# Transposing softmax weights in seven blocks of 128 keys over two heads instead of eight blocks of 112

## The chip, the cores and the metric

The kernel runs on one core of a Trainium2 chip. Its engines are named as in the profile: PE (TensorE, matrix products) with its weight loads PEld, DVE (VectorE), ACT (ScalarE), POOL (GpSimd) and SP (SyncE, which here only issues transfers). The metric is the device time of one launch in microseconds (us), where lower is better.

## The reference, cut to what matters

Attention over 4 batches of 12 heads with 448 tokens and 64 dimensions a head, then two MLP blocks. Everything is float32.

```python
q_n, k_n = (rmsnorm(q, g_q), rmsnorm(k, g_k))          # over the 64 dimensions of a head
scores = scale * np.matmul(q_n, k_n.transpose(0, 1, 3, 2))
scores = scores - np.max(scores, axis=-1, keepdims=True)
attn = np.exp(scores)
attn = attn / (np.sum(attn, axis=-1, keepdims=True) + 1e-09)
attn_out = np.matmul(attn, v)                          # (4, 12, 448, 64)
x = attn_out.transpose(0, 2, 1, 3).reshape(B, S, H * D)
# then: x + relu(layernorm(x) * g_ln @ w_ch1) @ w_ch2, and a gated MLP with a product over tokens
```

## The kernel before, in words

The program has three stages on the time axis: attention, the first MLP (`ph` and `pm` products, L781 and L804), and the gated MLP. Attention works on 24 pairs of heads. A head's 448 tokens are split in 4 chunks of 112 rows (`CP, NCH = 112, 4`): token 4p + c stands in row p of chunk c, for queries, keys and values alike.

For a pair i, numbered in the tile names, PE, ACT and DVE do this:

- `pk`, `pq` (L526): four transposes each bring the normalized k and q of both heads to 128 rows (2 heads of 64 dimensions) by 448 tokens; ACT copies them out as `kT`, `qT` (L535).
- `s` (L550): for each query chunk c, the scores of 112 queries against 448 keys, one product for each head, which run side by side on the two halves of PE's rows. DVE takes the row maximum (`nmx`, L556), ACT the exponential into `P`, one tile of 112 x 448 for each head and chunk, with the row sums (L560).
- `t` (L584): the weights `P` are transposed, so that keys lie on partitions. For each head j there are 4 blocks of 112 keys and 4 query chunks: 32 transposes for a pair, in 4 groups of 8 (`t00`, `t01`, `t10`, `t11`: first digit the half of the keys, second the head). Each group fills two PSUM banks and is copied out as `PT`, three groups by ACT (L114) and one by DVE (L594).
- `po` (L601): 8 products of v (112 keys x 64 dimensions) with `PT`, 4 key blocks for each head, the two heads side by side on the two halves of PE's columns.
- `px`, `x`, `pxT`, `y`: the result is copied (`OT`), transposed back, divided by the row sums on DVE (L640), kept for the layer norm's statistics (`lnst`), transposed again and copied to `y`.

POOL squares and normalizes the next pairs' q and k (`sq`, `kq`, L421 to L487). SP loads k, q (two pairs at a time) and v (L506, one transfer a pair into one of two `vr` buffers).

The code does not write the instructions out in a loop: `op(...)` records each step with a place number, an engine, an assumed cost and what it reads and writes, and `arrange` (L296) then emits them. PE's steps are emitted strictly in the order of their place numbers; the others go to whichever ready step comes first by the assumed times. The place numbers come from `ORDER` (the PE steps of a pair and how many pairs they run ahead or behind), `BEHIND` (places of the other engines' steps relative to those), and `EARLY`, single corrections by step and pair, which before exist for pairs 0 to 3 alone. PE changes between three ways of working: the full array (F: all transposes), two row halves (R: `s`) and two column halves (C: `po`). `FILL` (L69) adds products of the identity with itself ahead of some steps near the start, whose results are overwritten.

PSUM has three two-bank buffers `s` for `s` and `t`, and two one-bank buffers `x` for the rest.

Of the kernel before, what the change touches and what calls it, by code (L numbers as in the profile page):

```python
# [39 lines left out]
def attention_mlp_gated(ctx, tc, q, k, v, g_q, g_k, g_ln, w1, w2, w_in, w_sp, b_sp, w_out, out):  # L40
# [437 lines left out]
    def plan_norm(i, n0):  # L478
# [15 lines left out]
        for z, nm in enumerate(("k", "q")):  # L494
            hs = (2 * j, 2 * j + 1)
            r = [f"{nm}r{g}"] + [f"{x}{h}" for x in (f"{nm}r{g}_", f"rq{g}_{nm}") for h in hs]
            w = {"w": [f"kq{i}", f"kn{i}"], "new": "ws"} if z == 0 else {"w": [f"qn{i}"]}
            op(n0 + 2 * z, e, f, lambda nm=nm: norm(nm), r=r + ([f"kq{i}"] if z else []), **w)

    def plan_v(i, n0):  # L500

# [880 lines left out]
```

## Time and profile before

| what | value |
|---|---|
| median of 3 runs | 1213.06 us (1211.55 to 1213.32) |
| the profiled execution's own time | 1213.73 us |
| its span in the profile | 1211.9 us |
| busy in the span: PE, PEld | 1197.6 us, 1023.7 us |
| busy in the span: DVE, ACT, POOL | 765.8 us, 460.6 us, 301.9 us |
| granted PE clock over the run | 0.998 |

The span runs from the first instruction to the last. Busy time counts instructions that do work. PE's products are pipelined, and the end of one in the profile lies after the start of the next, so how fast PE goes is read from one group's start to the next one's, not from an instruction's own duration.

### The profile page before, as it was taken

Reading aid. Unit: us, or ns where it says so; the run is one execution under the profiler, and the core shown is the slowest. Engines: PE = TensorE matmul, PEld = TensorE weight load, DVE = VectorE, ACT = ScalarE, POOL = GpSimd, SP = SyncE. Lnnn points to the kernel's source line nnn. Section 1 sums busy time; section 2 is a strip of 40 time slices with the busy share of each in tenths; the row PEclk is TensorE's granted clock in tenths of the full one; section 3 lists DMA queues with packets and bytes.
Section 4 is the critical chain, followed back from the end, with each engine's and each line's share of the span. In section 5 each row is a group of like instructions: output and inputs, shape, how many; then the busy total and the mean of one; then the engine's idle time right before and its main releaser. Section 6 shows DMA issues by size and latency. Waiting matters only on the chain.

```text
span 1211.9 us, 16730 instructions
## 1 busy us (share of the span) xinstructions
PE 1197.6 (99%) x6568; PEld 1023.7 (84%) x6568; DVE 765.8 (63%) x1398; ACT 460.6 (38%) x918; POOL 301.9 (25%) x275
## 2 busy tenths in 40 slices
PE   8999999999999999999999999999999999999998
PEld 6565656657899999999999999999999988989888
DVE  6888898987888666665758576756445573241240
ACT  4788888997423222222213131322212031223122
POOL 4754767633111101010202010111111003140200
PEclk9999999999999999999999999999999999999999
DMA  4212112111214342323322223233010219102103
GB/s 111 74 54 78 53 54 67 60 42 42 78 53 145 116 133 67 130 77 114 104 87 93 90 104 104 104 109 101 27 52 2 103 67 324 46 1 75 39 1 92
DMA packets 59855, 99.26 MB, mean 82 GB/s; under 512 B 11584, under 2 KB 47808, under 8 KB 59520
## 3 DMA queue, kind: packets, MB, share of 16 engines
q1 hardware_dynamic: 59168, 95.44, 24.9%
q10 hardware_dynamic: 608, 2.75, 0.6%
q8 instruction: 52, 0.85, 0.3%
q14 instruction: 27, 0.22, 0.1%
HBM read 78.88 MB, written 19.30 MB: 81 GB/s over the span
## 4 chain that ended last, share of the span: by engine, by line
PE 91%; DVE 4%; ACT 2%; DMA 2%; POOL 1%; issue 0%; POOLq 0%; ACTq 0%; SPq 0%
PE ph L781 29%; PE pm L804 28%; PE s L550 5%; PE po L601 5%; PE gp L1042 5%; PE gv L888 5%; PE gu L936 5%; PE t L584 4%; PE gs L963 2%; ACT P L560 1%; DVE nmx L556 1%; DMA kr<-in_k_dram 1%; DVE y L812 1%; PE pq L526 1%; PE pxT L656 1%; PE px L635 1%
## 5 line engine op out<-in xcount | busy, mean ns | idle before, releaser
L804 PE MATMUL pm<-h,ws 128*128 128x448 f32 x1728 | 361.4, 362 | 0.0
L781 PE MATMUL ph<-xn,ws 128*128 128x448 f32 x1728 | 360.9, 362 | 0.3 <-DVE y L812 0.3
L804 PEld LDWEIGHTS pm<-h,ws 128*128 128x128 f32 x1728 | 323.8, 188 | 22.3 <-issue 0.7
L781 PEld LDWEIGHTS ph<-xn,ws 128*128 128x128 f32 x1728 | 323.8, 188 | 22.1 <-DVE y L812 0.5
L244 POOL TENSOR_TENSOR ws<-wc,ws 128x768 fp32r<-128x768 f32 x48 | 91.8, 1912 | 570.3 <-ACT ws L114 545.0
L812 DVE TENSOR_TENSOR y<-pm,y 128x448 f32<-128x448 f32 x318 | 176.2, 614 | 56.2 <-PE pm L804 56.2
L791 ACT ACTIVATE h<-ph 128x448 fp32r<-128x448 f32 x96 | 51.8, 539 | 256.0 <-PE ph L781 255.5
L796 DVE SCALAR_TENSOR_TENSOR h<-ph,h 128x448 fp32r<-128x448 f32 x96 | 59.6, 621 | 117.2 <-ACT h L791 116.2
L560 ACT ACTIVATE P<-s,nmx 112x448 f32<-112x448 f32 x192 | 119.3, 637 | 33.5 <-DVE nmx L556 31.3
L556 DVE TENSOR_REDUCE nmx<-s 112x2 f32<-112x896 f32 x96 | 101.2, 1083 | 22.2 <-PE s L550 22.0
L584 PE MATMUL t<-ident,P 112*112 112x112 f32 x768 | 88.9, 260 | 2.4 <-ACT P L560 1.8
L104 ACT ACTIVATE wc<-wr 128x768 f32<-128x768 f32 (+1 forms) x64 | 54.8, 859 | 94.0 <-DMA wr<-in_moe_w_ch_dram 49.3
L114 ACT ACTIVATE ws<-wc 128x768 fp32r<-128x768 f32 x48 | 40.5, 844 | 118.5 <-PE ph L781 92.0
L550 PE MATMUL s<-kT,qT 64*112 64x448 f32 x384 | 85.2, 563 | 0.0
L584 PEld LDWEIGHTS t<-ident,P 112*112 112x112 f32 x768 | 76.6, 133 | 7.6 <-ACT P L560 5.3
L601 PE MATMUL po<-PT,vr 112*64 112x448 f32 x384 | 77.6, 545 | 0.0
L105 DVE TENSOR_SCALAR wc<-wc 128x768 f32<-128x768 f32 (+1 forms) x64 | 40.6, 638 | 50.3 <-ACT wc L104 49.9
L114 ACT ACTIVATE PT<-t 112x896 f32<-112x896 f32 x72 | 66.2, 931 | 4.5 <-PE t L584 2.8
L601 PEld LDWEIGHTS po<-PT,vr 112*64 112x64 f32 x384 | 26.4, 136 | 47.2 <-issue 45.6
L107 DVE SCALAR_TENSOR_TENSOR wc<-wr,wc 128x768 int32<-128x768 int32 (+1 forms) x64 | 64.4, 1010 | 1.5
L108 DVE SCALAR_TENSOR_TENSOR wc<-wr,wc 128x768 uint32<-128x768 uint32 (+1 forms) x64 | 62.5, 977 | 1.6
L550 PEld LDWEIGHTS s<-kT,qT 64*112 64x112 f32 x384 | 30.6, 173 | 37.0 <-issue 21.9
(166 smaller groups left out, 1240.5 us busy)
## 6 DMA issues: line engine op xcount, KB each, us to landing
wr<-in_moe_w_ch_dram SPq DMA_DIRECT2D x48, 768.0 KB, 4.4
wr<-in_moe_w_in_dram SPq DMA_DIRECT2D x12, 512.0 KB, 3.7
win_dram<-wr SPq DMA_DIRECT2D x12, 512.0 KB, 2.6
vr<-in_v_dram SPq DMA_DIRECT2D x24, 224.0 KB, 2.7
kr<-in_k_dram SPq DMA_DIRECT2D x11, 448.0 KB, 4.0
qr<-in_q_dram SPq DMA_DIRECT2D x11, 448.0 KB, 4.7
wr<-in_moe_w_out_dram SPq DMA_DIRECT2D x4, 768.0 KB, 5.0
wout_dram<-wr SPq DMA_DIRECT2D x4, 768.0 KB, 3.2
```

The lines of the kernel that those rows point to most:

```text
L107: lambda: v.scalar_tensor_tensor(ci, hi, -0x40000000, ci, op0=ALU.bitwise_and, op1=ALU.bitwise_or),
L108: lambda: v.scalar_tensor_tensor(cu, lo.bitcast(U32), 29, cu, op0=ALU.logical_shift_right, op1=ALU.bitwise_or),
L114: nc.scalar.activation(d, s, AF.Copy)
L244: nc.gpsimd.tensor_tensor(t[:, 1], pl["c"], f32(t[:, 0]), op=ALU.subtract)
L550: nc.tensor.matmul(p[:CP, j, :S], pr["qT"][rows, c * CP : (c + 1) * CP], pr["kT"][rows], start=True, stop=True)
L556: nc.vector.tensor_reduce(t, pr["s", c][:CP, :, :S], axis=AX.X, op=ALU.max, negate=True)
L560: nc.scalar.activation(t, pr["s", c][:CP, j, :S], AF.Exp, bias=pr["m", c][:, j : j + 1], scale=1.0, accum_out=pr["sum"][:, j, c : c + 1],)
L584: nc.tensor.transpose(p[:CP, e, c * CP : (c + 1) * CP], pr["P", j, c][:, kc * CP : (kc + 1) * CP], ident[:CP, :CP])
L601: nc.tensor.matmul(pr["po"][j * D : (j + 1) * D, :S], raw["v", i][:, j, kc, :], pr["PT", kc // 2, j][:, kc % 2], start=(kc == 0), stop=(kc ...
L781: nc.tensor.matmul(hid[u, b][0][:, :S], s1[:, a, kk, :], xn[b][:, c, kk, :], start=(kk == 0 and m == 0), stop=(kk == NK - 1 and m == 2),)
L804: nc.tensor.matmul(po[:, :S], s2[:, a, m * P : (m + 1) * P], hs[:, c, :], start=(first and e == 0), stop=(last and e == 2),)
L812: nc.vector.tensor_tensor(y[b][:, m, :], po[:, :S], y[b][:, m, :], op=ALU.add)
```

## The change

The keys of a pair's two heads are put side by side: `P` becomes one tile of 112 queries x 896 keys for each chunk, where each head's exponential fills one half. The 896 keys are cut in 7 windows of 128 instead of 8 of 112: windows 0 to 2 belong to the first head, 4 to 6 to the second, and window 3 holds the first head's last 64 keys and the second head's first 64. A pair takes 28 transposes instead of 32, each from 112 x 128 to 128 x 112. They stand in four groups: windows 0 and 1, 5 and 6, 2 and 4 (this one copied by DVE), and window 3 alone (a copy of 448 columns instead of 896, by ACT).

`po` keeps its 8 products: three windows for each head, and window 3 once for each head, with v rows that are zero where the keys are the other head's. The zeros are written once, into two `vr` buffers that stay; after that a pair's v is loaded by 4 transfers instead of 1, in rows of 64 numbers instead of 256. So that keys come in token order, the four transposes of k write every fourth column of `pk`. The `P` pool has 7 tiles of double size instead of 14. `ORDER`, `BEHIND`, `FILL` and the places of `plan_rms` and `plan_norm` get other numbers, and `EARLY` now has corrections for all 24 pairs.

```diff
-    FILL = {"pq0": 22, "s0_3": 5, "s0_0": 4, "pk1": 12, "s1_0": 3}
+    FILL = {"pq0": 22, "s0_1": 3, "s0_3": 15, "t0_0_0": 3, "pk2": 4}
...
-    ORDER = "po-1 s3+1 pq+2 t00 px-1 t11 pk+2 t10 pxT-1 t01 s2+1 s0+1 s1+2".split()
+    ORDER = "po-1 s3+1 pk+2 t10 px-1 t01 pq+2 t11 t00 pxT-1 s2+1 s0+1 s1+2".split()
...
-            raw["v", i] = ap["vraw"].tile([CP, 2, NCH, D], F32, tag="vr", name=f"vr{i}")
-            nc.sync.dma_start(
-                raw["v", i].rearrange("p h c d -> p h (c d)"),
-                v[b, 2 * hp : 2 * hp + 2].rearrange("h (p c) d -> p h (c d)", c=NCH),
-            )
-
+            t = raw["v", i] = vrs[i % 2]
+            for j in range(2):
+                of = v[b, 2 * hp + j]
+                nc.sync.dma_start(t[j * D : (j + 1) * D, j, 3], of[(1 - j) * 3 * P : (1 - j) * 3 * P + D])
+                nc.sync.dma_start(t[:, j, :3], of[j * D : j * D + 3 * P].rearrange("(w p) d -> p w d", p=P))
...
-                    p[:, c * CP : (c + 1) * CP],
+                    p[:, c:S:NCH] if nm == "k" else p[:, c * CP : (c + 1) * CP],
...
+        WINDOWS = {(0, 0): (0, 1), (0, 1): (5, 6), (1, 0): (2, 4), (1, 1): (3,)}
...
-            for e in range(2):
-                kc = 2 * half + e
+            for e, w in enumerate(WINDOWS[half, j]):
                 for c in range(NCH):
                     nc.tensor.transpose(
-                        p[:CP, e, c * CP : (c + 1) * CP], pr["P", j, c][:, kc * CP : (kc + 1) * CP], ident[:CP, :CP]
+                        p[:, e, c * CP : (c + 1) * CP], pr["P", c][:, w * P : (w + 1) * P], ident[:CP, :CP]
                     )
...
-            for kc in range(NCH):
+            for z in range(NCH):
                 for j in range(2):
+                    w = 3 if z == NCH - 1 else 4 * j + z
                     nc.tensor.matmul(
                         pr["po"][j * D : (j + 1) * D, :S],
-                        raw["v", i][:, j, kc, :],
-                        pr["PT", kc // 2, j][:, kc % 2],
-                        start=(kc == 0),
-                        stop=(kc == NCH - 1),
+                        raw["v", i][:, j, w - 4 * j if z < NCH - 1 else 3],
+                        pr["PT", w],
+                        start=(z == 0),
+                        stop=(z == NCH - 1),
                     )
```

The instructions on PE for the transposes of pair 12, where the first number after a tile's name is the pair. Before, this group (second half of the keys, second head) has eight rows, between `px11` and `pk14`:

```order
L635 MATMUL px11_2243<-ident_64,OT11_2218 112x128 x4
L584 MATMUL t12_1_1_2254<-ident_64,P12_0_1_2197 112x112
L584 MATMUL t12_1_1_2254<-ident_64,P12_1_1_2052 112x112
L584 MATMUL t12_1_1_2254<-ident_64,P12_2_1_2188 112x112
L584 MATMUL t12_1_1_2254<-ident_64,P12_3_1_2101 112x112
L584 MATMUL t12_1_1_2254<-ident_64,P12_0_1_2197 112x112
L584 MATMUL t12_1_1_2254<-ident_64,P12_1_1_2052 112x112
L584 MATMUL t12_1_1_2254<-ident_64,P12_2_1_2188 112x112
L584 MATMUL t12_1_1_2254<-ident_64,P12_3_1_2101 112x112
L526 MATMUL pk14_2267<-ident_64,kq14_1961 128x112 x4
```

In the changed kernel the group of that name holds window 3 alone and has four rows; it now stands last of the four groups, behind `pxT11`:

```order
L737 MATMUL pxT11_2208<-ident_64,x11_2167 128x112 x4
L658 MATMUL t12_1_1_2217<-ident_64,P12_0_2123 128x112
L658 MATMUL t12_1_1_2217<-ident_64,P12_1_1965 128x112
L658 MATMUL t12_1_1_2217<-ident_64,P12_2_2114 128x112
L658 MATMUL t12_1_1_2217<-ident_64,P12_3_2019 128x112
L619 MATMUL s13_2_2227<-kT13_2009,qT13_2059 112x448 x2
```

The other three groups keep eight rows, with results of 128 x 112 instead of 112 x 112. Over the program the `t` rows fall from 768 to 672; the other products of PE are as many as before (its identity fills 47 instead of 46), and PE changes its way of working 104 times between the first and the last of the attention's steps instead of 103. From the end of attention on, PE's order is the same in both.

ACT's rows around the copies of pair 12, before:

```order
L114 ACTIVATE PT12_0_0_2272<-t12_0_0_2232 112x896
L535 ACTIVATE kT14_2293<-pk14_2267,gk_c_69 128x448
L114 ACTIVATE PT12_1_0_2304<-t12_1_0_2274 112x896
L114 ACTIVATE PT12_0_1_2315<-t12_0_1_2295 112x896
L114 ACTIVATE y1_1540<-pxT11_2288 128x448
```

and in the changed kernel, where the third copy has half the columns:

```order
L114 ACTIVATE PT12_0_1_2194<-t12_0_1_2176 128x896
L604 ACTIVATE qT14_2213<-pq14_2189 128x448
L114 ACTIVATE PT12_0_0_2223<-t12_0_0_2196 128x896
L114 ACTIVATE PT12_1_1_2234<-t12_1_1_2217 128x448
L114 ACTIVATE y1_1506<-pxT11_2208 128x448
```

DVE keeps one copy of 896 columns for each pair. At the start of the program PE's rows up to the second pair's first scores were these before (`pq0` to `s1_0`):

```order
L73 MATMUL s0_3_221<-ident_64 128x128 x5
L550 MATMUL s0_3_221<-kT0_214,qT0_210 112x448 x2
L550 MATMUL s0_2_233<-kT0_214,qT0_210 112x448 x2
L550 MATMUL s0_1_239<-kT0_214,qT0_210 112x448 x2
L73 MATMUL s0_0_254<-ident_64 128x128 x4
L550 MATMUL s0_0_254<-kT0_214,qT0_210 112x448 x2
L73 MATMUL pk1_300<-ident_64 128x128 x12
L526 MATMUL pk1_300<-ident_64,kq1_288 128x112 x4
L526 MATMUL pq1_324<-ident_64,kq1_288 128x112 x4
```

and are these in the changed kernel:

```order
L73 MATMUL s0_1_229<-ident_64 128x128 x3
L619 MATMUL s0_1_229<-kT0_222,qT0_219 112x448 x2
L619 MATMUL s0_0_239<-kT0_222,qT0_219 112x448 x2
L619 MATMUL s0_2_245<-kT0_222,qT0_219 112x448 x2
L73 MATMUL s0_3_282<-ident_64 128x128 x15
L619 MATMUL s0_3_282<-kT0_222,qT0_219 112x448 x2
L595 MATMUL pk1_305<-ident_64,kq1_258 128x112 x4
L595 MATMUL pq1_312<-ident_64,kq1_258 128x112 x4
L73 MATMUL t0_0_0_331<-ident_64 128x128 x3
```

The fills ahead of the fourth scores rise from 4 to 15, the 12 ahead of `pk1` are gone, and two groups of pair 0's transposes now come before the second pair's scores instead of behind two of them.

## Rows read from the trace of the kernel before

**Rows 1.** Windows of the program: busy time of each engine and granted clock.

```profile
core 0: us, PE busy (x) PEld busy (x) DVE busy (x) ACT busy (x) POOL busy (x), PEclk, DMA share, GB/s
0.00:46.00 46.00, 38.39 (x254) 28.28 (x254) 32.93 (x78) 25.70 (x59) 25.85 (x35) 0.96 0.37 96
46.00:303.00 257.00, 255.60 (x1783) 158.41 (x1784) 219.95 (x473) 219.21 (x521) 149.58 (x145) 1.00 0.20 58
312.00:1212.00 900.00, 894.99 (x4491) 830.87 (x4489) 506.79 (x833) 213.45 (x337) 126.19 (x96) 1.00 0.27 89
```

**Rows 2.** Chain of work that ended last, 100 to 126 us: start, us, what.

```profile
105.45 3.16 PE po L601 x16
108.61 0.94 PE s L550 x4
...
111.29 0.77 PE t L584 x8
112.06 0.38 PE pk L526 x4
112.44 0.77 PE t L584 x8
113.21 0.38 PE pxT L656 x4
113.59 0.77 PE t L584 x8
114.36 2.44 PE s L550 x12
116.80 3.16 PE po L601 x16
```

**Rows 3.** The same chain, products with v: the second pair's and the 22nd's.

```profile
48.48 3.16 PE po L601 x16
...
280.94 3.16 PE po L601 x16
```

**Rows 4.** Groups of instructions by form, 46 to 303 us: count, busy, mean.

```profile
L584 PE MATMUL t<-ident,P 112*112 112x112 f32 x704 | 81.4, 260 | 1.2 <-ACT P L560 1.0
L114 ACT ACTIVATE PT<-t 112x896 f32<-112x896 f32 x66 | 60.9, 932 | 4.3 <-PE t L584 2.5
L594 DVE COPY PT<-t 112x896 f32<-112x896 f32 x23 | 24.9, 1085 | 1.7 <-PE t L584 0.9
L114 ACT ACTIVATE OT<-po 128x448 f32<-128x448 f32 x22 | 12.5, 567 | 0.0
```

**Rows 5.** Weight loads on PE in order of time, 157 to 161 us.

```profile
157.86 0.82 PEld L584 LDWEIGHTS t<-ident,P 112*112 112x112 f32 x8
158.64 0.43 PEld L526 LDWEIGHTS pk<-ident,kq 112*128 112x128 f32 x4
159.03 0.81 PEld L584 LDWEIGHTS t<-ident,P 112*112 112x112 f32 x8
159.79 0.43 PEld L656 LDWEIGHTS pxT<-ident,x 112*128 112x128 f32 x4
160.18 0.81 PEld L584 LDWEIGHTS t<-ident,P 112*112 112x112 f32 x8
```

**Rows 6.** Transfers by line: count, KB each, median us to landing.

```profile
vr<-in_v_dram SPq DMA_DIRECT2D x24, 224.0 KB, 2.7
wr<-in_moe_w_spatial_dram SPq DMA_DIRECT2D x16, 56.0 KB, 2.3
```

**Rows 7.** PE in order of time near the start, idle time before in brackets.

```profile
16.75 2.08 PE L73 MATMUL s<-ident 128*128 128x128 f32 x8 [2.02 <-ACT P L560]
...
20.38 2.94 PE L73 MATMUL pk<-ident 128*128 128x128 f32 x24
```

**Rows 8.** Waits, 46 to 303 us: who for whom, us in total, times, longest.

```profile
PE t L584 <- ACT P L560: 1.0, 2, 0.7
...
ACT P L560 <- DVE nmx L556: 20.1, 21, 2.1
...
DVE nmx L556 <- PE s L550: 19.5, 27, 1.8
```

More of the change, by code (lines that the diff above doesn't have):

```diff
@@ L276, in at @@
     def at(nm, i):
-        return 8 * i + AT[nm] + EARLY.get((nm, i), 0)
+        return 8 * i + AT[nm] + EARLY.get(nm, {}).get(i, 0)
     def op(n, eng, us, fn, r=(), w=(), new=None, mode=None):
@@ L497, in plan_norm @@
             w = {"w": [f"kq{i}", f"kn{i}"], "new": "ws"} if z == 0 else {"w": [f"qn{i}"]}
-            op(n0 + 2 * z, e, f, lambda nm=nm: norm(nm), r=r + ([f"kq{i}"] if z else []), **w)
+            op(
+                n0 + 2 * z + EARLY.get(("KQkq", "KQqn")[z], {}).get(i, 0), e, f, lambda nm=nm: norm(nm), r=r + ([f"kq{i}"] if z else []), **w,
+            )
+    vrs = []
     def plan_v(i, n0):
@@ L504, in load @@
         def load():
-            raw["v", i] = ap["vraw"].tile([CP, 2, NCH, D], F32, tag="vr", name=f"vr{i}")
-            nc.sync.dma_start(
-                raw["v", i].rearrange("p h c d -> p h (c d)"),
-                v[b, 2 * hp : 2 * hp + 2].rearrange("h (p c) d -> p h (c d)", c=NCH),
-            )
+            t = raw["v", i] = vrs[i % 2]
[3 more added lines that the diff above has]
+                nc.sync.dma_start(t[:, j, :3], of[j * D : j * D + 3 * P].rearrange("(w p) d -> p w d", p=P))
+        if i < 2:
+            vrs.append(ap["vraw"].tile([P, 2, NCH, D], F32, tag=f"vr{i}", name=f"vr{i}"))
+            for j in range(2):
+                nc.gpsimd.memset(vrs[i][(1 - j) * D : (2 - j) * D, j, 3], 0.0)
         dma(n0 - 2, 229, load, w=[f"vr{i}"], new="vr")
@@ L574, in plan_pair @@
             for j in range(2):
-                r = ["s" + o, "nmx" + o, f"ssum{i}"]
-                op(at(f"P{c}", i), "ACT", 0.62, lambda c=c, j=j: s_exp(c, j), r=r, w=[f"P{o}_{j}"], new="P")
+                r = ["s" + o, "nmx" + o, f"ssum{i}"] + ["P" + o] * j
+                w, new = ([f"P{o}_1"], None) if j else (["P" + o, f"P{o}_0"], "P")
+                op(at(f"P{c}", i), "ACT", 0.62, lambda c=c, j=j: s_exp(c, j), r=r, w=w, new=new)
+        WINDOWS = {(0, 0): (0, 1), (0, 1): (5, 6), (1, 0): (2, 4), (1, 1): (3,)}
+        DVE_COPY = (1, 0)
         def t_pe(half, j):
@@ L611, in plan_pair @@
                 o, n = f"{i}_{half}_{j}", at(f"t{half}{j}", i)
-                r = [f"P{i}_{c}_{j}" for c in range(NCH)]
-                op(n, "PE", 0.77, lambda half=half, j=j: t_pe(half, j), r=r, w=["t" + o], new="s", mode="F")
-                eng, us = ("DVE", 1.08) if half and j else ("ACT", 0.92)
+                r = [f"P{i}_{c}{x}" for c in range(NCH) for x in ["", "_0", "_1"] if x != f"_{1 - j}" or half]
+                us = 0.385 if half and j else 0.77
+                op(n, "PE", us, lambda half=half, j=j: t_pe(half, j), r=r, w=["t" + o], new="s", mode="F")
+                eng = "ACT" if (half, j) != DVE_COPY else "DVE"
+                us = (0.56, 0.56) if half and j else (0.92, 1.08)
+                us = us[eng == "DVE"]
                 op(at(f"PT{half}{j}", i), eng, us, lambda half=half, j=j, eng=eng: t_out(half, j, eng), r=["t" + o], w=["PT" + o], new="PT")
@@ L647, in ln_stats @@
         def ln_stats(cs):
-            if hp == 0 and 0 in cs:
+            if b not in lnst:
                 lnst[b] = lnp.tile([CP, NCH, NPAIR, 6], F32, tag="lnst", name=f"lnst{b}", bufs=3)
@@ L658, in xT_act @@
         def xT_act():
-            if hp == 0:
+            if b not in y:
                 y[b] = y_a.tile([P, NK, S], F32, tag="y", name=f"y{b}")
```

38 lines of the change are left out of this document (25 added, 13 removed), and 59 rows, old and new, of tables (BEHIND, EARLY).

## Prediction

> **What bounds the kernel now.** I read the windows of the program first [rows 1]. From 46 to 303 us, where attention runs steadily, PE is busy 255.60 of 257.00 us at a granted clock of 1.00, while DVE and ACT are busy 219.95 and 219.21 us, about 85% each. From 312 us to the end PE is busy 894.99 of 900.00 us. So PE sets the time nearly everywhere, and only the first 46 us hold much else (38.39 us busy there, part of it fills). A busy PE is not proof, since its durations overlap, so I then took the chain that ended last and read distances between starts. Between two products with v that follow each other without a gap it holds PE's work alone: 105.45 to 116.80 us, 11.35 us for one pair [rows 2]. Over 20 pairs, from the second pair's product with v at 48.48 us to the 22nd's at 280.94 us, the mean is 232.46 / 20 = 11.62 us [rows 3]. Three batches end in that stretch, each with eight more transposes for the layer norm, at 0.38 us for four like those of pk [rows 2]: 3 x 0.76 = 2.3 us. 20 x 11.35 + 2.3 = 229.3 us, so PE's waits are worth about 232.5 - 229.3 = 3.2 us in 20 pairs. That is the whole that a better order could win in the steady part. Whatever takes work off PE in each pair is therefore worth its full size, as long as the engines behind it keep pace.
>
> **The transposes.** A group of eight takes 0.77 us on the chain [rows 2], 0.096 us for one. (The 260 ns mean of one [rows 4] is latency and must not be multiplied.) Four fewer for each of 24 pairs are 96 x 0.096 = 9.2 us. That needs a transpose with 128 weight columns to go as fast as today's with 112. The trace has such transposes: pk and pxT load 112 x 128, and the next group starts 0.39 us after the first of four (158.64 to 159.03, 159.79 to 160.18), against 0.76 or 0.78 us for eight of the 112 x 112 kind [rows 5]. So the pace is the same, 0.096 to 0.0975 us, set by the 112 columns that move, which the change keeps. At 0.0975 us the saving is 24 x (32 x 0.096 - 28 x 0.0975) = 8.2 us. Bounds: 8.2 to 9.2 us; I take 9.2.
>
> One rule speaks against this. The Trainium skill, "TensorE: Matmul & The Clock Gate", section "LDWEIGHTS (loading the stationary operand)", says that a weight load takes its number of columns divided by 1.2 in ns, whatever the rows. By it 128 columns are 106.7 ns, more than the 96 ns pace, and if loads set the pace the pair would save 32 x 0.096 - 28 x 0.1067 = 0.08 us, 2 us in all, an estimate. The groups in [rows 5] disagree with loads being the limit; the trace decides, and the case is a rival below.
>
> **The copies.** Each pair has one ACT copy of 448 columns instead of 896. The nearest row for the short one is OT at 567 ns, for the long one PT at 932 ns [rows 4]: 24 x 0.365 = 8.8 us less on ACT. DVE keeps its copy of 1085 ns. Both lie beside PE and win nothing by themselves, but they decide who is next: in the steady part, shortened by about 22 x 0.384 = 8.4 us, ACT would be busy (219.2 - 8.0) / 248.6 = 85% as now, DVE 219.95 / 248.6 = 88%. Copies to 128 partitions instead of 112 cost what the row of OT, which has 128, shows.
>
> **Products with v.** Still eight, and 448 columns move through each. 128 key rows instead of 112 lengthen nothing that moves. The last two take one window for both heads, with zeros in v. Zero, with PE's own pairing of the two heads kept, since heads still alternate.
>
> **Keys in token order.** The four transposes of k write every fourth column of the bank. No row of before shows a strided result. Below: nothing, if each column is a write of its own anyway. Above: four places for each one, 96 transposes x 3 x 0.096 = 27.6 us. The only neighbour is the plain pk at 0.38 us for four [rows 2]. I take zero and carry the upper end as a rival.
>
> **Loads of v.** 96 transfers instead of 24, in rows of 256 bytes instead of 1024. SP issues three more for each pair. A transfer of 224 KB now lands 2.7 us after issue, and one of 56 KB that the code cuts into runs of 128 bytes in 2.3 us [rows 6]. So four transfers of 16 or 96 KB should land within four times 2.7 = 10.8 us even one behind the other. They can start when the pair two before has done its product with v and must be there two periods less one product later, 2 x 11.6 - 3.2 = 20 us [rows 2, 3]. Hidden; k and q queue behind them on SP, with the same wait for PE ahead as before. If the cover were gone, each us beyond 20 would be paid in each of 22 pairs. The Trainium skill's "DMA: Bandwidth & Descriptors", section "Specifications", gives 512 bytes as the least size for full rate, so these rows fall below it; no run here shows rows of 256 bytes.
>
> **P in seven tiles.** Same bytes. A tile comes free when both heads are transposed instead of one, so ACT may run slightly less far ahead; ACT waits for DVE's maxima (20.1 us) and not for tiles [rows 8]. Zero. The four small memsets on POOL come before POOL has anything to do: zero. One more change of PE's way of working, 104 instead of 103: zero.
>
> **The order.** It is new everywhere. Steady part: it can return at most the 3.2 us above. PE waits little for named work there (1.0 us for ACT's exponentials [rows 8]), so I give it 0.5 us. Start: before, PE waits 2.02 us for ACT at 16.75 us, runs four fills (8 records, 2.08 us at the lower clock), and later 12 fills in 2.94 us [rows 7]. The changed kernel has 15 fills where the four stood and none of the 12. At 0.52 us for a fill 11 more cost up to 5.7 us, at 0.245 us 2.7 us; the 12 gone give back 2.94 us, and two groups of pair 0's transposes fill what was waiting. Both ends: 3 us lost to 3 us won; I take 0.5 us won. After attention PE's order is the same, so the later stages begin earlier by what is saved and keep their length.
>
> **Sum.** The profiled execution took 1213.73 us with a span of 1211.9 us, 0.05% above the median of 1213.06 us, so the sum carries over. 1213.06 - 9.2 - 0.5 - 0.5 = 1202.9, said as 1203 us; its own range 1201 to 1206 us.
>
> **Rivals.**
> - *More is won*: the new order also takes the remaining 2.7 us of steady waits and 2 to 3 us of the start. 1197 to 1201 us. For it: the corrections now reach every pair. Against: PE's named waits are small.
> - *DVE takes over as the bound*: it goes in order and would be 88% busy, with small steps for q and k between the maxima. Each late maximum holds ACT's exponentials, and these the transposes. For it: ACT already waits 20.1 us for maxima. Against: DVE itself waits 19.5 us for PE's scores [rows 8], which come sooner now. If 0.15 to 0.3 us a pair is lost, 3 to 7 us of the 9.2 go: 1206 to 1211 us.
> - *The change saves PE nothing* because weight loads set the pace: at 128/112 of 0.096 us, 28 transposes take 24 x 28 x 0.110 = 73.7 us, as 32 do now. With ACT's relief alone, 1211 to 1213 us. The rows of pk and pxT [rows 5] speak against it; the skill's page named above would put it there too (estimate).
> - *Strided writes of pk are slow*, the case that ends slower: place, the four transposes of k in each pair; price, 9.2 us for each further 0.096 us a transpose. It decides at twice the pace, 0.19 us, where it eats the whole saving; at four times the time is 1203 + 27.6 = 1231 us. Nothing in the trace speaks for it.
> - *The start loses*: the 15 fills hold the fourth scores and all behind them longer than I think, by 5 us or more: 1208 to 1214 us.
>
> **Chances.** Forecast 0.60, more won 0.12, DVE 0.15, no saving 0.05, strided writes 0.04, the start 0.04. The range 1198.5 to 1209.5 us holds the forecast, three quarters of "more" (0.09) and four fifths of the DVE case (0.12): 0.81. A measurement of this kernel can tell about 0.2% (2.4 us) from no change, so faster means under 1210.6 us: 0.60 + 0.12 + 0.13 from the DVE case = 0.85. Within 0.2%: no saving 0.05, the rest of DVE 0.02, the start 0.03 = 0.10. Slower: 0.05.
>
> **What would show it.** Right: groups of eight `t` still 0.77 us apart on the chain and the group of window 3 0.385 us; a pair without layer-norm transposes at 11.35 - 0.385 = 10.97 us between products with v; 20 pairs in about 224 us; ACT's copy of 448 columns near 570 ns; from the end of attention on about 900 us as before; v landed long before it is waited for. Wrong: `t` at 0.107 us or more apiece, `pk` groups over 0.38 us to the next start, DVE named as what PE's transposes wait for, or the second pair's product with v later than 48.5 us by more than 2 us.

## The result

The changed kernel is slower: 1218.48 us (median of 5 runs, 1216.52 to 1220.21) against 1211.60 us for the kernel before on the same chip (5 runs, 1211.22 to 1213.32), a ratio of 1.0053 [1.0041, 1.0065]. The forecast was 1203 us, in a range of 1198.5 to 1209.5 us. The profiled execution has a span of 1216.7 us at a mean granted PE clock of 0.997, 4.8 us more than the one profiled before. The medians lie 6.9 us apart, because the execution that was profiled before took 1213.73 us, 2.1 above its own median.

### The profile page after: what moved, and what is told of

Same layout as the page of the kernel before. It is cut to its first block, busy times and chain, and to the rows that moved or that the text cites. A ratio compares the mean times of both kernels' runs of the same rounds, so it can differ in the third digit from the quotient of the medians.

```text
span 1216.7 us, 16674 instructions
## 1 busy us (share of the span) xinstructions
PE 1192.2 (98%) x6474; PEld 1015.2 (83%) x6474; DVE 781.3 (64%) x1398; ACT 452.5 (37%) x918; POOL 302.3 (25%) x279
## 4 chain that ended last, share of the span: by engine, by line
PE 89%; DVE 7%; ACT 2%; issue 1%; POOL 1%; DMA 0%; SPq 0%; DVEq 0%; ACTq 0%; POOLq 0%
PE ph L862 28%; PE pm L885 28%; PE s L619 5%; PE gp L1123 5%; PE gv L969 5%; PE gu L1017 5%; PE po L679 4%; PE t L658 4%; PE gs L1044 2%; DVE nmx L625 2%; ACT P L630 1%; PE pxT L737 1%; PE pk L595 1%; PE gs L1056 1%; DVE rs L708 1%
## 5 line engine op out<-in xcount | busy, mean ns | idle before, releaser
L885 PEld LDWEIGHTS pm<-h,ws 128*128 128x128 f32 x1728 | 323.6, 187 | 22.5 <-issue 0.7
L625 DVE TENSOR_REDUCE nmx<-s 112x2 f32<-112x896 f32 x96 | 100.8, 1080 | 19.4 <-PE s L619 19.2
L658 PE MATMUL t<-ident,P 112*128 112x112 f32 x672 | 76.7, 261 | 6.6 <-DVE PT L671 3.7
L658 PEld LDWEIGHTS t<-ident,P 112*128 112x128 f32 x672 | 67.0, 141 | 12.9 <-ACT P L630 6.2
L679 PE MATMUL po<-PT,vr 128*64 128x448 f32 x384 | 77.5, 545 | 0.0
L105 DVE TENSOR_SCALAR wc<-wc 128x768 f32<-128x768 f32 (+1 forms) x64 | 40.2, 631 | 49.4 <-ACT wc L104 49.0
L679 PEld LDWEIGHTS po<-PT,vr 128*64 128x64 f32 x384 | 25.4, 136 | 49.0 <-issue 45.7
L619 PEld LDWEIGHTS s<-kT,qT 64*112 64x112 f32 x384 | 29.8, 172 | 40.6 <-issue 16.5
L1123 PE MATMUL gp<-wout,gg 128*128 128x384 f32 x336 | 58.7, 334 | 0.0
```

The costliest lines, as they stand in the source:

```text
L619: nc.tensor.matmul(p[:CP, j, :S], pr["qT"][rows, c * CP : (c + 1) * CP], pr["kT"][rows], start=True, stop=True)
L625: nc.vector.tensor_reduce(t, pr["s", c][:CP, :, :S], axis=AX.X, op=ALU.max, negate=True)
L658: nc.tensor.transpose(p[:, e, c * CP : (c + 1) * CP], pr["P", c][:, w * P : (w + 1) * P], ident[:CP, :CP])
L679: nc.tensor.matmul(pr["po"][j * D : (j + 1) * D, :S], raw["v", i][:, j, w - 4 * j if z < NCH - 1 else 3], pr["PT", w], start=(z == 0), sto ...
L885: nc.tensor.matmul(po[:, :S], s2[:, a, m * P : (m + 1) * P], hs[:, c, :], start=(first and e == 0), stop=(last and e == 2),)
L1123: nc.tensor.matmul(po[:, :half_n], gt[g][:, a, i * P : (i + 1) * P], W["out"][:, g, e, half * half_n : (half + 1) * half_n], start=(g == 0 ...
```

## The profile after

The windows of the changed kernel, which answer to [rows 1]; the last row is a window of its own, from the seventh pair's product with v to the 17th's (ten pairs).

```profile
core 0: us, PE busy (x) PEld busy (x) DVE busy (x) ACT busy (x) POOL busy (x), PEclk, DMA share, GB/s
...
46.00:303.00 257.00, 245.49 (x1676) 145.00 (x1675) 233.05 (x474) 211.01 (x519) 151.81 (x148) 1.00 0.22 58
...
105.10:230.90 125.80, 114.48 (x778) 67.26 (x776) 116.49 (x229) 99.20 (x244) 77.25 (x77) 1.00 0.22 56
```

The same ten pairs of the kernel before:

```profile
105.40:223.00 117.60, 116.70 (x818) 71.42 (x816) 103.38 (x230) 102.56 (x245) 79.14 (x78) 1.00 0.22 60
```

PE is idle for 257.00 - 245.49 = 11.5 us of the steady part instead of 1.4, nearly all of it in these ten pairs (125.80 - 114.48 = 11.3 us, before 0.9). POOL and ACT have no more to do there, but DVE is busy for 13 us longer, with the same work but for the order.

The chain that ended last (start, us, what), which answers to [rows 2] and [rows 3]: products with v, and between the first two of them three groups of transposes:

```profile
49.45 3.16 PE po L679 x16
...
56.44 0.38 PE t L658 x4
...
58.30 0.77 PE t L658 x8
59.06 0.38 PE pk L595 x4
...
82.78 3.16 PE po L679 x16
...
93.74 3.16 PE po L679 x16
...
287.36 3.16 PE po L679 x16
```

Eight `t` still take 0.77 us, the four of window 3 take 0.38, and so do the four of `pk` that write every fourth column (0.53 right behind scores, as `pxT` does there). Where nothing is late, a pair takes 93.74 - 82.78 = 10.96 us: the 10.97 us of the forecast. So the transposes saved what they should. Yet the 20 pairs take 287.36 - 49.45 = 237.9 us instead of the 224 forecast and 232.5 before [rows 3]. By stretches, against the kernel before: to the second pair +1.0 us; to the seventh (105.09 us, before 105.45 [rows 2]) -1.3; the ten pairs +8.2; from there to the last pair (307.1 us, before 302.4) -3.2; the rest +0.1. That is the 4.8 us.

The groups of ACT's copies, 46 to 303 us, which answer to [rows 4], and the larger transfers of v, to [rows 6]:

```profile
L114 ACT ACTIVATE PT<-t 128x896 f32<-128x896 f32 x44 | 40.3, 927 | 3.4 <-PE t L658 3.0
...
L114 ACT ACTIVATE PT<-t 128x448 f32<-128x448 f32 x23 | 13.0, 563 | 0.0
```

```profile
vr<-in_v_dram SPq DMA_DIRECT2D x48, 96.0 KB, 2.3
```

The waits in the ten pairs (who for whom, us in total, times, longest), to be read beside [rows 8]:

```profile
ACT P L630 <- DVE nmx L625: 21.9, 15, 4.6
...
PE t L658 <- DVE PT L671: 3.7, 3, 1.9
PE s L619 <- ACT P L630: 3.2, 2, 2.4
```

ACT waits for maxima for 21.9 us in the ten pairs (9.3 before), and PE, after that, for ACT's exponentials. Why the maxima are late stands in DVE's queue. DVE in order of time in the worst pair, which takes 14.4 us from 142.2 us on (start, us, line, operation, out<-in):

```profile
137.94 2.07 DVE L837 SCALAR_TENSOR_TENSOR xn<-lnx,gl_c,xn 128x448 fp32r<-128x448 f32 x1
139.94 0.41 DVE L496 TENSOR_REDUCE ss<-sq7q 112x8 f32<-112x256 f32 x1
140.38 0.67 DVE L506 TENSOR_SCALAR ss<-ss 112x32 f32<-112x32 f32 x1
141.08 0.18 DVE L82 TENSOR_SCALAR rr<-ss 112x32 int32<-112x32 int32 x1
141.30 1.01 DVE L88 SCALAR_TENSOR_TENSOR rt<-rr 112x32 f32<-112x32 f32 x1
142.34 0.96 DVE L89 TENSOR_TENSOR rt<-rt,ss 112x32 f32<-112x32 f32 x1
143.34 1.86 DVE L90 SCALAR_TENSOR_TENSOR rr<-rt,rr 112x32 f32<-112x32 f32 x1
145.23 0.19 DVE L88 SCALAR_TENSOR_TENSOR rt<-rr 112x32 f32<-112x32 f32 x1
145.34 3.08 DVE L625 TENSOR_REDUCE nmx<-s 112x2 f32<-112x896 f32 x3
```

POOL at the same time:

```profile
141.09 1.16 POOL L820 TENSOR_TENSOR lnx<-lnx,lnbc 128x448 f32<-128x448 f32 x1
...
143.33 0.72 POOL L486 TENSOR_TENSOR sq8k<-sq8k 112x256 f32<-112x256 f32 x1
144.01 1.14 POOL L817 TENSOR_TENSOR lnx<-y,lnbc 128x448 f32<-128x448 f32 x1
```

The instruction at L88 takes 0.19 us at 145.23 and 1.01 us at 141.30, where it ends (142.31) as POOL's instruction ends (142.25). The one at 143.34 ends at 145.20, with the second of two POOL instructions (145.15). Four of the small steps here end with POOL's instruction, or with the one after it, and are called held below; L82 and the second L88, which start within 0.01 us of one of POOL's, take no longer than alone. Eight instructions whose shortest records add up to 2.0 us take 145.34 - 137.94 = 7.4, the three maxima behind them start at 145.34, and ACT has waited 4.6 us when it goes on.

In the ten pairs four groups of DVE make up the 13 us (29.5 against 16.2). The first fence is the changed kernel, the second the kernel before (L445 is L506, L627 is L708, L756 is L837); after the bar busy us and mean ns of one.

```profile
L837 DVE SCALAR_TENSOR_TENSOR xn<-lnx,gl_c,xn 128x448 fp32r<-128x448 f32 x9 | 11.7, 1300 | 0.6 <-ACT xn L834 0.6
...
L708 DVE TENSOR_SCALAR rs<-ssum 112x8 f32<-112x8 f32 x10 | 8.1, 809 | 1.6 <-ACT P L630 1.4
...
L90 DVE SCALAR_TENSOR_TENSOR rr<-rt,rr 112x32 f32<-112x32 f32 x15 | 5.9, 393 | 0.2
...
L506 DVE TENSOR_SCALAR ss<-ss 112x32 f32<-112x32 f32 x5 | 3.8, 761 | 0.0
```

```profile
L756 DVE SCALAR_TENSOR_TENSOR xn<-lnx,gl_c,xn 128x448 fp32r<-128x448 f32 x9 | 7.3, 806 | 0.0
...
L627 DVE TENSOR_SCALAR rs<-ssum 112x8 f32<-112x8 f32 x10 | 4.8, 478 | 0.6 <-ACT P L560 0.2
L90 DVE SCALAR_TENSOR_TENSOR rr<-rt,rr 112x32 f32<-112x32 f32 x15 | 2.8, 188 | 0.2
...
L445 DVE TENSOR_SCALAR ss<-ss 112x32 f32<-112x32 f32 x5 | 1.3, 254 | 0.1
```

At the start, 15 fills stand ahead of pair 0's fourth scores, after a wait for ACT (before: 2.08 us after 2.02 [rows 7]):

```profile
18.65 6.41 PE L73 MATMUL s<-ident 128*128 128x128 f32 x30 [4.16 <-ACT P L630]
```

## The experiments

**Theory A**, formed from these rows: the new order puts DVE's small SBUF steps where POOL is at work; DVE is held, its maxima come late, and PE waits. Its rivals: the blocks, the order as such, or DVE's own work is to blame. "Held" below is the time of DVE's records beyond the shortest record of the same line and shape, summed where it is over 0.15 us. All ratios are to runs of the kernel before on the same chip; the runs lie on several chips, where that kernel's median was 1211.60 to 1212.48 us, so times of different rows compare to about 1 us. The ten pairs are those above, PE idle is their length less PE's busy time in their window, and the clock is the granted one of that window.

| run | us | ratio | ten pairs, us | PE idle | DVE held | ACT waits for maxima | clock |
|---|---|---|---|---|---|---|---|
| before | 1211.60 | 1 | 117.6 | 0.9 | 12.6 | 9.3 | 1.00 |
| changed | 1218.48 | 1.0053 | 125.8 | 11.3 | 28.2 | 21.9 | 1.00 |
| e1_blocks_old_order | 1245.62 | 1.0276 [1.0262, 1.0290] | 130.7 | 11.9 | 17.9 | 21.6 | 0.99 |
| e2_new_order_old_blocks | 1243.40 | 1.0261 [1.0247, 1.0275] | 131.4 | 9.6 | 21.0 | 21.9 | 0.96 |
| e3_dve_short_copy | 1237.42 | 1.0212 [1.0197, 1.0226] | 125.5 | 8.3 | 19.2 | 16.1 | 0.99 |
| e4_less_pool_after | 1202.47 | 0.9917 [0.9904, 0.9931] | 114.6 | 1.5 | 10.8 | 9.3 | 1.00 |
| e4_less_pool_before | 1208.82 | 0.9971 [0.9959, 0.9982] | 115.3 | 0.0 | 5.7 | 6.6 | 1.00 |
| e5_four_fills | 1215.23 | 1.0021 [1.0012, 1.0030] | 125.6 | 7.8 | 26.6 | 20.4 | 0.97 |
| e6_no_fold_short | 1240.81 | 1.0231 [1.0214, 1.0248] | 127.0 | 8.4 | 11.6 | 16.5 | 0.97 |
| e7_no_fold_after | 1212.17 | 0.9998 [0.9989, 1.0007] | 118.5 | 4.1 | 16.5 | 16.3 | 1.00 |
| e10_no_fold_same_order | 1218.86 | 1.0048 [1.0035, 1.0060] | 124.6 | 8.4 | 23.5 | 20.4 | 0.97 |
| e10_no_fold_before | 1211.11 | 0.9993 [0.9984, 1.0001] | 117.6 | 1.2 | 12.3 | 8.3 | 1.00 |
| e11_no_add_after | 1218.00 | 1.0042 [1.0029, 1.0056] | 127.9 | 9.4 | 24.8 | 22.2 | 0.96 |
| e11_no_add_before | 1211.74 | 0.9985 [0.9971, 1.0000] | 117.7 | 1.0 | 10.3 | 9.2 | 1.00 |
| e9_no_fold_four_fills | 1212.35 | 0.9997 [0.9988, 1.0006] | 120.3 | 6.1 | 22.4 | 17.2 | 1.00 |
| e12_no_add_four_fills | 1215.06 | 1.0019 [1.0007, 1.0031] | 126.3 | 9.1 | 24.3 | 22.5 | 0.97 |
| e13_no_add_no_fold | 1208.28 | 0.9959 [0.9944, 0.9974] | 117.7 | 3.7 | 14.2 | 14.6 | 1.00 |
| e14_maxima_first | 1223.17 | 1.0087 [1.0073, 1.0100] | 125.1 | 9.4 | 17.2 | 17.4 | 0.99 |
| e15_one_refinement | 1212.33 | 1.0003 [0.9995, 1.0012] | 122.7 | 8.2 | 21.6 | 18.9 | 1.00 |

### Blocks and order apart (e1, e2)

The numbers of `ORDER`, `BEHIND`, `EARLY`, `FILL` and the steps' places, exchanged between the kernels: e1 has the new blocks in the old order, e2 the old blocks in the new order.

```diff
-    ORDER = "po-1 s3+1 pk+2 t10 px-1 t01 pq+2 t11 t00 pxT-1 s2+1 s0+1 s1+2".split()
+    ORDER = "po-1 s3+1 pq+2 t00 px-1 t11 pk+2 t10 pxT-1 t01 s2+1 s0+1 s1+2".split()
...
```

> The seven blocks, the loads of v and the one tile for both heads, with the numbers of before for every place (ORDER, BEHIND, EARLY, FILL and the places of the squares and norms). Theory A (the new order lets small DVE steps fall behind POOL's steps, the blocks themselves are worth what was forecast): 1202 to 1206 us, 0.993 of before. Theory B (the new order loses by its own waits, not by POOL): the same here. Theory C (the blocks themselves cost, by the groups that need both heads or the tile of double size): 1212 us or more.

> The kernel before with only the order's numbers of the change (ORDER, BEHIND, EARLY, FILL, places of squares and norms); eight blocks of 112, one load of v. Theories A and B: slower than the changed kernel by the 9 us of transposes, 1223 to 1229 us. Theory C: near before, 1210 to 1214 us.

e1 took 1245.62 us (ratio 1.0276 [1.0262, 1.0290]), e2 1243.40 us (1.0261 [1.0247, 1.0275]): both far above what theories A and B gave. Theory C's open range for e1 (1212 us or more) holds it, but the same theory put e2 at 1210 to 1214 us, so it fails too. In e1 PE waits 18.2 us for DVE's copies of `PT`, once for 5.4 us. The orders are fitted to their blocks. Which half of the change loses can't be read from an exchange of halves, and an order alone moves this kernel by some 30 us.

### Less work on POOL, nothing moved (e4)

For both kernels, with every row of PE, ACT and DVE in its place and POOL's in the same order, only smaller (`w` is 32 for the first three batches, so part of the computation is left out):

```diff
-                (nc.vector if eng == "DVE" else nc.gpsimd).tensor_tensor(sq, t, t, op=ALU.mult)
+                h = D if eng == "DVE" else D // 2
+                (nc.vector if eng == "DVE" else nc.gpsimd).tensor_tensor(sq[:, :, :h], t[:, :, :h], t[:, :, :h], op=ALU.mult)
...
-                eng.tensor_tensor(t, t, ln["bc"][:, 1], op=ALU.add)
+                eng.tensor_tensor(t[:, :w], t[:, :w], ln["bc"][:, 1, :w], op=ALU.add)
```

> The changed kernel, same order, with less work on POOL: squares of q and k over 32 of 64 dimensions, their fold over one column, the second layer-norm step of the first three batches over 32 of 448 tokens; this part of the computation is left out. POOL is busy some 60 us less in attention. Theory A: DVE's time behind POOL falls from about 48 us to under 25 us and the time to 1206 to 1212 us. Theory B: 1216 to 1219 us.

> The same cut of POOL's work in the kernel before (the same part of the computation left out), as a control for what less POOL work gives when DVE has room. Theory A: 1 to 4 us less than before, since DVE there is held 27 us but PE waits only some 3 us in the steady part. Theory B: the same, so that the two cuts win alike.

The changed kernel gains 16.0 us, more than the 6 to 12 expected, the one before 3.4 (1212.20 to 1208.82), and the change is then worth 6.4 us. Of the 16.0 us, 11.2 lie in the ten pairs and 4.1 ahead of the second pair's product with v (45.3 us instead of 49.4). From there 20 pairs take 226.0 us, where the forecast had 224. The steady part of the changed one:

```profile
46.00:303.00 257.00, 255.45 (x1736) 155.50 (x1733) 218.10 (x490) 215.17 (x524) 100.06 (x145) 1.00 0.23 60
```

DVE, whose own work is untouched, is busy for 15 us less although the window holds more of its instructions (490 for 474), and PE is back at 255.45 of 257. That POOL's results come late is no rival there: in the changed kernel DVE waits for them 2.1 us in all, in the whole steady part, and ACT 0.7. So what was lost in the steady part was lost through POOL's work beside DVE's. At the start the two are not apart, since PE itself waits 1.4 us for a `kq` of POOL there.

### The holding by itself (e8)

`forms()` issues ten kinds of DVE instruction once each:

```diff
...
+        for _ in range(8):
+            forms()
+        d.tensor_copy(pb, wide)
+        for _ in range(160):
+            nc.gpsimd.tensor_tensor(pc, pa, pb, op=ALU.mult)
+        for _ in range(8):
+            forms()
```

> Nothing of the reference is computed: ten kinds of DVE instruction of the kernel run eight times each, first with POOL idle, then while POOL runs 160 multiplications of 128 x 448 in SBUF one after the other. Theory A (a DVE instruction with operands in SBUF is held while POOL runs one): the small steps on SBUF (sum, product, the two-step forms, the second half of xn) take their 0.1 to 0.8 us with POOL idle, and up to one POOL instruction more, 0.5 to 1 us on the mean, with POOL at work; the forms that read PSUM and the reductions stay within 0.1 us. Rival (they only looked long because their records overlap others): the means agree within 0.1 us in both parts.

DVE's groups with POOL idle (10 to 37 us), and with POOL at work (39 to 80 us):

```profile
L74 DVE COPY pt<-big 128x896 f32<-128x896 f32 x8 | 8.7, 1092 | 0.3
...
L71 DVE SCALAR_TENSOR_TENSOR w<-wide,col,w__73 128x448 f32<-128x448 f32 x7 | 4.4, 633 | 0.0
...
L69 DVE SCALAR_TENSOR_TENSOR s<-small,sr 112x32 f32<-112x32 f32 x7 | 1.4, 193 | 0.0
```

```profile
L71 DVE SCALAR_TENSOR_TENSOR w<-wide,col,w__73 128x448 f32<-128x448 f32 x8 | 10.7, 1340 | 0.0
L74 DVE COPY pt<-big 128x896 f32<-128x896 f32 x8 | 8.7, 1092 | 0.3
L67 DVE TENSOR_SCALAR s<-small 112x8 f32<-112x8 f32 x7 | 5.5, 790 | 0.0
...
L69 DVE SCALAR_TENSOR_TENSOR s<-small,sr 112x32 f32<-112x32 f32 x8 | 2.5, 312 | 0.0
```

xn's second half goes from 633 to 1340 ns, the small sum from 161 ns (its usual record with POOL idle) to 790; copies from PSUM, reductions (412 and 406 ns), statistics and the reciprocal (196 ns in both) don't change. Of five SBUF steps in a row the first and the last are held, by 0.63 and 0.71 us where POOL's instruction takes 1.14, and the three short ones between them hardly (one of eight at L69, 1.14 us). So the theory holds for some steps, and not, as it was put, for every small one. The steps that were held, and the reductions that never were, agree with the Trainium skill, "SBUF — State Buffer", section "Who interferes with whom": DVE and GpSimd share one pair of SBUF ports, which one instruction holds to its end; a DVE instruction with two SBUF inputs, or one in a two-port mode, needs it, a reduction never does. By that rule the product and the two-step form (L68, L69) right behind the sum, with two SBUF inputs each, would need it too, and in the seven rounds that begin with POOL at work they take 0.18 and 0.19 us as with POOL idle. The rounds lie 5.1 us apart in one fixed phase to POOL's instructions, so this is one case seen seven times.

### DVE's and POOL's share (e3, e6, e7, e10)

e3 gives DVE the copy of 448 columns and ACT three long ones; e7 leaves POOL's fold of the squares out and lets DVE reduce 64 columns; e6 does both. In these three the planner (`arrange`) moves rows as well, DVE's most of all. e10 leaves out the folds with no row moved, in both kernels; its edit is the second one below.

```diff
-        DVE_COPY = (1, 0)
+        DVE_COPY = (1, 1)
```

```diff
-            nc.gpsimd.tensor_tensor(sq[:, :, :z], sq[:, :, :z], sq[:, :, z:], op=ALU.add)
-            st[nm, h] = sq[:, :, :z]
```

> DVE takes the copy of 448 columns instead of one of 896, ACT takes the three long ones: about 24 x 0.5 = 12 us less on DVE, 24 x 0.365 = 8.8 us more on ACT, POOL as it is. Theory A (DVE is late, because its small instructions are held while POOL runs, and PE waits for what DVE then delivers late): DVE has slack to take up what is held, and the time falls to 1209 to 1214 us, though DVE is held for as long as in the changed kernel. Rival (the waits are not DVE's, the order itself is poor): 1217 to 1220 us. Second rival (ACT, with three long copies, is now what PE waits for): above 1222 us.

> Both: no fold on POOL (DVE reduces 64 columns), and DVE takes the copy of 448 columns. Theory A: DVE's longer reductions are paid by the shorter copy, and about half of the holding is gone: 1203 to 1209 us, faster than both kernels. Rival (the order itself is poor, no engine's lateness matters): 1216 to 1220 us. Second rival (ACT becomes what PE waits for): 1210 to 1218 us, with waits of PE named for ACT's copies.

> POOL's fold of the squares is left out, DVE reduces 64 columns instead of 32; the output is the same. POOL has 44 x 0.73 = 32 us less to do, DVE 44 x 0.26 = 11 us more. Theory A (DVE is held by POOL's instructions): what is held falls by about half, some 12 us, which pays for DVE's longer reductions where POOL's work lies closest; the time is 1208 to 1215 us. Rival (DVE's own busy time is the limit, whatever POOL does): 1220 to 1226 us.

> The changed kernel without POOL's folds, with no instruction of any engine moved: POOL has 44 x 0.73 = 32 us less, DVE's 44 reductions take 0.26 us more each, 11 us. Theory A (what DVE is held for is what the change lost): about 12 to 15 us less are held, half of that shows: 1208 to 1214 us. Rival (DVE's own work is the limit): 1220 to 1226 us.

> The same in the kernel before, again with no instruction moved. Theory A: DVE was held for half as long there and had slack, so at most 2 us are won and up to 5 lost to DVE's longer reductions: 1210 to 1217 us. Rival (less work on POOL helps any kernel as much): as many us are won as in the changed kernel.

e3 took 1237.42 us (1.0212 [1.0197, 1.0226]) and e6 1240.81 (1.0231 [1.0214, 1.0248]). PE's first wait in e3 is

```profile
PE t L658 <- ACT PT L114: 8.7, 8, 3.9
```

So its second rival holds: the copies that PE waits for come too late from ACT, and the run says nothing of theory A. e6 lies above all three of its ranges: DVE is held for 11.6 us in the ten pairs, less than in the kernel before, and PE is idle for 8.4 all the same; in the steady part it waits 8.6 us for copies of DVE and 6.5 for copies of ACT. Little holding alone does not make an order good. e7 came out as theory A had it (1212.17, held 28.2 to 16.5 us), but with rows moved, so the folds alone are not shown to do it. e10 did not: 1218.86 us, as the rival of a limit by DVE's own work would nearly have it. Held time fell by only 4.7 us in the ten pairs, DVE's longer reductions took it up, and the clock (next) cost 1.7 us of PE's busy time. The kernel before gained 0.07%, which can't be told from nothing.

### The step held most (e11), and a clock that falls

```diff
-            nc.vector.tensor_scalar(pr["rs"], pr["sum"], 1e-9, None, op0=ALU.add)
...
-            nc.vector.reciprocal(pr["rs"], pr["rs"])
+            nc.vector.reciprocal(pr["rs"], pr["sum"])
```

> The changed kernel without the step that adds 1e-9 to the sums of the exponentials (a sum is at least 1, where 1e-9 changes nothing in float32); the reciprocal reads the sums directly, nothing else is moved. In the changed kernel that step takes 14.3 us in 24 pairs, 4.0 of it its own and 10.3 held. Theory A (DVE's time, held or its own, is what PE waits for; reciprocals were never held): 14 us less on DVE, most of it shows: 1206 to 1212 us. Rival (the reciprocal is held in its place): 1215 to 1218 us. Second rival (DVE's time does not matter): 1218 us.

> The same in the kernel before. Theory A: DVE had slack there, and PE waits for 3.2 us in 20 pairs in all: 1209 to 1212 us. Rival (it helps any kernel as much): as many us are won as in the changed kernel.

1218.00 us: a step of 14.2 us taken from DVE, and nothing won; DVE waited for scores instead (22.0 us in the steady part, 11.8 in the changed kernel). Two things ate it. Held time passes on: without the step the next SBUF step is held (the xn that took 2.07 us above takes 3.28), so the ten pairs hold 24.8 us instead of 28.2, where the step alone had held 6.5. And one wait of PE got longer, 3.46 us instead of 2.41, with this in e11 (PE in order of time, then windows with the granted clock behind the busy times):

```profile
146.91 1.84 PE L619 MATMUL s<-kT,qT 64*112 64x448 f32 x4 [3.46 <-ACT P L630]
```

```profile
144.00:146.00 2.00, 0.00 (x0) 0.00 (x0) 2.00 (x3) 0.48 (x1) 1.56 (x2) 1.00 0.26 58
146.00:148.00 2.00, 1.09 (x4) 0.45 (x4) 2.00 (x4) 1.96 (x7) 0.00 (x0) 0.54 0.25 56
148.00:150.00 2.00, 2.00 (x10) 1.32 (x8) 1.97 (x8) 2.00 (x8) 0.00 (x0) 0.50 0.00 0
...
154.00:156.00 2.00, 2.00 (x16) 1.29 (x15) 0.36 (x2) 2.00 (x4) 2.00 (x3) 1.00 0.00 0
```

After PE had stood for 3.46 us the granted clock was 0.50, the lower level (1.2 GHz), and 1.00 again only in the window from 154 us on; after 2.41 us in the changed kernel it stayed at 1.00. PE's busy time in the ten pairs rose from 114.48 to 118.47 us, 4.0 us for the same work, while its idle time fell by 1.9. The same shows in e5 (117.81), e12 (117.18) and e10 (116.21): where the clock falls, a gain is hidden. The length of the wait alone does not decide it: the clock fell to 0.50 in e11 a second time at 228.1 us after a wait of 1.92 us, and in e5 at 135.1 and 210.2 us after waits of 1.76 and 1.45 us, while the changed kernel kept 1.00 through waits of 1.77, 2.41, 1.45 and 1.93 us.

### The place of the held steps (e14, e15)

**Theory B** of these two runs (another than that of e1, e2 and e4): what counts is that held steps stand ahead of the maxima. e14 moves only DVE's reciprocal-root steps and xn, behind maxima; e15 removes steps of the clusters.

```diff
+            if getattr(fn, "late", False):
+                waiting.append((i, fn))
+                continue
+            while before[i] & {d for d, f in waiting}:
+                waiting.pop(0)[1]()
+            if eng == "DVE":
+                maxima = any(e.startswith("nmx") for e in w)
+                for _ in range(min(2, len(waiting)) if passed and not maxima else 0):
+                    waiting.pop(0)[1]()
...
```

```diff
-            else:
+            elif z < 5 or g == 0:
                 st["steps", h][z - 1]()
```

> On DVE alone, the steps of the reciprocal roots and the second half of xn wait until maxima that stood behind them are issued, at most two for each later instruction, and none between a copy of PT and the next maxima unless something needs them; no row of PE, ACT or POOL is moved, and the work is the same. Theory B (it is the place: held steps in front of the maxima are what makes PE wait): 4 us or more are won, 1208 to 1214 us, and the pairs that took 13 to 14.4 us come nearer to 12. Rival (what DVE has to do in all decides): 1217 to 1220 us. Second rival (the steps now hold the copies of PT): above 1220 us, with PE waiting for PT.

> From the third pair on two of three refinements of the reciprocal roots for q and k are left out (the roots are less exact), 66 DVE instructions of 0.26 to 0.42 us with what holds them, 22 us in all; no instruction left is moved. Theory B (held steps in the clusters ahead of the maxima make PE wait): most of the 12 us of the steady part come back, 1206 to 1212 us, where removing 14 us of DVE's time behind the maxima won nothing. Rival (POOL or the order itself makes PE wait): 1216 to 1219 us.

e14 is slower still, 1223.17 us. The pair of 14.4 us came down to 10.9, but others rose, and PE's first waits are

```profile
PE t L676 <- DVE PT L689: 4.8, 3, 2.3
PE pxT L755 <- DVE x L739: 3.1, 3, 1.8
```

With that theory B falls: steps moved off the maxima hold the copies and `x`, for which PE waits as well (e14's second rival). The start is 2.5 us later too. e15 took 1212.33 us, just above what theory B gave: 6 us won, but of these the ten pairs hold 3.1, not most of their 12, and the start 2.9.

### The start, and all gains together (e5, e9, e12, e13)

```diff
-    FILL = {"pq0": 22, "s0_1": 3, "s0_3": 15, "t0_0_0": 3, "pk2": 4}
+    FILL = {"pq0": 22, "s0_1": 3, "s0_3": 4, "t0_0_0": 3, "pk2": 4}
```

> Four fills ahead of pair 0's fourth scores instead of fifteen. Theory (the fills hold the start, whose first product with v is 4.5 us and whose second is 1.0 us later than before): the second pair's product with v comes 1 to 3 us earlier and the time falls by as much, to 1215 to 1217 us. Rival (what follows the fills would wait for ACT and DVE anyway): 1218 to 1219 us. Second rival (without the fills TensorE's clock is granted later, and the start is slower): above 1220 us.

> The changed kernel without folds and with four fills instead of fifteen ahead of pair 0's fourth scores. If the two losses are apart, they add up: 3 us less than without the folds alone, 1205 to 1211 us. If the start only moves waiting from one place to another: as without the folds alone.

> Without the step of adding 1e-9, and four fills in place of fifteen. If the losses of the start and of the steady part are apart: 3 us less than without the step alone, 1203 to 1209 us, faster than both kernels.

> Without the step, with four fills, and with the squares' folds left out in the planner's own new order (the one that took 1212 us with all else as in the changed kernel). If all three add up: 1200 to 1206 us, not far above the forecast of 1203 us. If the holding that is left is DVE's slack already: as with the step and the fills alone.

e5: 1215.23 us, 3.2 less. Its fills take 1.36 us instead of 6.41, and the second pair's product with v comes at 44.8 us instead of 49.4:

```profile
18.25 1.36 PE L73 MATMUL s<-ident 128*128 128x128 f32 x8 [3.82 <-ACT P L630]
```

e9 (e10 with four fills) gives 1212.35 us, 6.5 less than e10, more than the start alone: where PE waits 3.52 us in e10 it waits 0.67 in e9, and the clock stays at 1.00. Why four fills at the start shorten that wait was not tried. It misses its range (1205 to 1211 us) by 1.4. e12 gives 1215.06, 2.9 less than e11, as expected of the difference, but above its range and no faster than e5. e13, the fills, no folds in the planner's new order and no sum, gives 1208.28 us: faster than both kernels, 0.41% [0.26, 0.56] under the one before, 10.2 us under the changed one, and short of its 1200 to 1206.

## Why the prediction was wrong

- *The transposes* (-9.2 us): right. Undisturbed pairs take 10.96 us, 10.97 forecast, and from the 17th pair on the changed kernel gains 3.2 us on the one before. The rivals of slow weight loads and of strided writes of `pk` are dead with it: the groups of `t` and `pk` take 0.77 and 0.38 us as before.
- *The copies*: ACT's short copy takes 563 ns (forecast near 570), the long one 927. What failed here is the reckoning "DVE 219.95 / 248.6 = 88%", which takes DVE's busy time over from the old order as a constant. It was 233.05 of 257 us, 91%, and 116.49 of 125.8, 93%, in the ten pairs. DVE's durations depend on what POOL does at that moment: the summed hold in the ten pairs went from 12.6 to 28.2 us with the same instructions.
- *The order* (-0.5 us for the steady part): this is the term that failed, and it was wrong in sign. It was bounded by what a better order could win (3.2 us), with no bound on what it could lose. The ten pairs were 12.3 us over the forecast (125.8 against 117.6 - 3.8 - 0.3 = 113.5), out of 15.0 us by which the whole span was over it. e4 gives back 11.2 us of them by thinning POOL's work alone; e7 and e13 give back 7 to 8 with POOL lightened and rows moved.
- *DVE takes over as the bound* (0.15): the right path, maxima late and ACT's exponentials behind them, and one of the signs named for a wrong forecast came, `t` waiting for DVE (3.7 us in the ten pairs). Its price was wrong: 0.15 to 0.3 us a pair, where the ten pairs cost 1.2. Of POOL as the reason why DVE is late it says nothing. The rival that ended slower was sought in `pk` and should have been this one.
- *The start* (-0.5 us): +2.2 us against the forecast by the second pair's product with v (49.4 against 48.5 - 0.5 - 2 x 0.38 = 47.2). Fifteen fills took 6.41 us at the lower clock, and e5 shows that 11 of them cost 4.6 us there and 3.2 at the end: inside the 2.7 to 5.7 us of the prediction, but nothing that waited was gained for it. They are not all: e4 keeps the fifteen fills and comes 4.1 us earlier there.
- *v, P in seven tiles, the later stages*: right. v lands in 2.3 us and PE waits for none of it; from the last product with v on the rest is as long as before within 0.1 us.

What stays open: how the loss divides between single held steps. e4 shows that POOL's work beside DVE is the cause as a whole in the steady part. Taking one held step away moved the hold to the next (e11), moving them moved the wait (e14), removing some 22 us of them won 6 us, 3.1 of them in the ten pairs (e15), and a fall of the clock hid part of four results (e5, e10, e11, e12). No run had the new order with small steps that cannot be held.

## What to carry to other kernels

Where DVE and POOL run side by side, a DVE duration from the old profile is a price only for the old order: look for records of one shape with two lengths, sum the excess, and ask whether the new order puts them beside POOL's work and ahead of what PE waits for. A term for "new order" needs a bound on the losing side as well, and here an engine at 88% that goes in order had less slack than it seemed. When an experiment that takes work off an engine wins nothing, look at the granted clock and at which instruction now carries the wait before the theory is given up.

## What was not expected of the hardware

A DVE instruction can be held over several POOL instructions in a row. The longest such record is in e3 (DVE, then POOL in order of time):

```profile
279.96 4.72 DVE L708 TENSOR_SCALAR rs<-ssum 112x8 f32<-112x8 f32 x1 [1.88 <-ACT P L630]
```

```profile
278.14 2.24 POOL L817 TENSOR_TENSOR lnx<-y,lnbc 128x448 f32<-128x448 f32 x2
280.33 2.24 POOL L820 TENSOR_TENSOR lnx<-lnx,lnbc 128x448 f32<-128x448 f32 x2
282.51 1.05 POOL L548 TENSOR_TENSOR kq<-qr,rr 112x512 f32<-112x512 f32 x1
283.51 2.22 POOL L817 TENSOR_TENSOR lnx<-y,lnbc 128x448 f32<-128x448 f32 x2
```

An instruction of 0.16 us took 4.72 us, from inside the second POOL instruction shown until the first of the last two ended. In e8, with POOL's queue always full, no hold was longer than one POOL instruction; what makes the difference was not tried. POOL is held as well: in e8 its instruction takes 1.13 us, and 1.39 where it starts just before a held `xn` of DVE ends (POOL from 44.64 us, `xn` from 43.60 to 45.04). And PE's clock: the granted clock fell to 0.50 after a single wait of 1.76 us in e5, and stayed at 1.00 through one of 2.41 us in the changed kernel.
